# Attention on two head pairs at a time: scores in 64x64 quarters of the array, beside the value products

## The chip, the cores and the metric

The kernel runs on one core of a Trainium2 chip. The metric is device microseconds of that core, the median of the runs of one build. Besides the timed runs there is one profiled execution of the kernel before, from which every row below is taken.

## What is computed

Windowed attention over 4 batches, 8 heads, 576 positions and 64 dimensions a head, then two expert layers, all in float32:

```python
scores = scale * np.matmul(q, k.transpose(0, 1, 3, 2))
mask = (rel >= 0) & (rel < window)            # window = 64
attn = np.exp(scores - max); attn = attn / (sum + 1e-9)
x = np.matmul(attn, v)                        # to [2304 tokens, 512]
h = x @ w_in                                  # 512 -> 2048
x = g(h) @ w_out                              # g piecewise quadratic, 2048 -> 512
h = x @ w_in2                                 # 512 -> 1024
h = h * softmax(h); h = layer_norm(h) * g_ln
out = h @ w_out2                              # 1024 -> 512
```

Here `rel` is query position less key position, so a query sees itself and the 63 keys before it.

## The kernel before

**Attention.** The 2304 tokens are 12 tiles of 192 (`TT`), three to a batch. A tile has four head pairs (`NP`); one tile and one head pair is a group `g`, 48 in all, worked on in order. A tile has three blocks of 64 queries (`QB`); each block sees 128 keys, its own 64 and the 64 before it. The first block of a batch sees only 64 (`first(t, i)`). A group goes through six steps:

- `load_qk` loads queries and keys of one group as 32x32 pieces, four DMAs for each, and `st_qkt` transposes them on VectorE: the keys of both heads go to `kT` (128 partitions, 64 for each head), the queries to `q_diag`, which holds for each query block 64 columns of head 0 in the upper 64 partitions and 64 of head 1 in the lower, and zeros elsewhere. (For the first 12 groups both go through TensorE instead.)
- `st_s` makes the scores of both heads in one product a block: 128 rows of `q_diag` (half of them zeros) against 128 columns of `kT`. VectorE adds the mask and takes the maximum, ScalarE the exponential with its sum.
- `st_norm` divides by the sum. `st_t` transposes the probabilities on TensorE, and ScalarE copies them to SBUF (`pT`).
- `st_v` multiplies by the values: for each block and head a product whose output has 64 partitions, head 0 in the upper and head 1 in the lower half of `ps_x`. ScalarE rounds the result into `xh`, VectorE keeps the rest in `xl`.

**First expert layer.** Blocks `j` of 384 tokens (two tiles), six of them, with 16 steps `f` each. `moe_h` multiplies 12 times into `ps_h` (hidden columns of step `f`), `moe_g` to `moe_g3` make the nonlinearity on ScalarE and VectorE, and `moe_y` multiplies 12 times into four accumulators `acc`, two steps later. All of these products have 384 columns over the full array ("ordinary products" below).

**How they are woven.** Attention runs ahead of the expert layer: each step `f` calls `slot` twice, and `slots` is a generator that yields between the attention's steps. Up to group `GB` = 16 it has one loop, from `GB + 1` on another; both take four slots, two steps `f`, a group. Block 0 of the expert layer takes groups 7 to 16, blocks 1 to 4 take the rest, and the last block runs beside the second layer's start. From block 1 on, `at_bank` and `h_bank` take PSUM banks from one ring of four, so a bank that one step takes must have been read by whoever used it four bank requests earlier. Weights of the first layer are loaded, converted and split during block 0; those of the second layer are converted in blocks 0 to 4. The framework then orders the instructions of each engine from the program's order and its own costs, so the order on an engine is not that of the code.

**What is quoted below.** Float32 products are recorded as two passes, so three score products (`x3`) are six records in the trace; transposes are recorded once.

Of the kernel before, what the change touches and what calls it, by code (L numbers as in the profile page):

```python
# [8 lines left out]
F32 = mybir.dt.float32  # L9
F32R = mybir.dt.float32r  # L10
# [10 lines left out]
def kernel(  # L21
# [28 lines left out]
    NG = NTILES * NP  # L50
    NST = 5
    G0, F0, NC, NQ, NV = 6, 2, 4, 6, 7

    const = ctx.enter_context(tc.tile_pool(name="const", bufs=1))
    dram = ctx.enter_context(tc.tile_pool(name="dram", bufs=1, space=DRAM))
# [51 lines left out]
    def as_f32(a):  # L107
        return a.bitcast(F32)
# [139 lines left out]


    NPE = 3 * NP  # L250
    qn, kn, qk, vw, qT, kT, xh, xl = {}, {}, {}, {}, {}, {}, {}, {}
    sc, pr, sums, pT = {}, {}, {}, {}

# [3 lines left out]
    def load_qk(g):  # L257
        t, hp = divmod(g, NP)
        b, tl = divmod(t, TPB)
        back = 64 if tl else 0  # L260
        if g < NPE:
            for src, dst, tag, r0, n in (
                (q, qn, "wih", tl * TT, TT // 2),
                (k, kn, "wil", tl * TT - back, (TT + back) // 2),
            ):
                for r in range(2):
                    if t < 2:
                        a = w_p.tile([128, 512], F32, tag=f"{tag}{14 - 2 * t + r}", name="qkn")
                    else:
                        a = at_p.tile([128, 512], F32, tag="qk", bufs=5, name="qkn")  # L270
                    dst[t, r] = a[0:n, :]
            for h0, h1 in ((0, 2), (2, H)) if t == 0 else ((0, H),):
                for src, dst, r0, n in ((q, qn, tl * TT, TT // 2), (k, kn, tl * TT - back, (TT + back) // 2)):
                    for r in range(2):
                        nc.sync.dma_start(
                            out=dst[t, r].rearrange("p (h d) -> p h d", h=H)[:, h0:h1],
                            in_=src[b, h0:h1, r0 + r * n:r0 + r * n + n, :].rearrange("h p d -> p h d"),
                        )
            return
        a = at_p.tile([128, 14, 32], F32, tag="qk", bufs=5, name="qk")  # L280
        for src, r0, m0 in ((q, tl * TT, 0), (k, tl * TT - back, 6)):
            n = tl * TT + TT - r0
            for x in range(2):
                s_ = src[b, 2 * hp + x, r0:r0 + n, :].rearrange("(m j) (e i) -> e j m i", j=32, i=32)
                for e in range(2):
                    p0 = 64 * x + 32 * e
                    nc.sync.dma_start(out=a[p0:p0 + 32, m0:m0 + n // 32, :], in_=s_[e])
        qk[g] = a
# [10 lines left out]
            vw[t, i] = w  # L299


    q_diag = [at_p.tile([128, QB, 2, 64], F32, bufs=1, name=f"q_diag{z}") for z in range(2)]
    for z in q_diag:
        nc.vector.memset(z, 0.0)

    def st_qkt(g):
        t, hp = divmod(g, NP)
        qt = qT[g] = q_diag[g % 2]
        kt = kT[g] = at_p.tile([128, TT + 64], F32, tag="kT", name="kT")
        if g >= NPE:  # L310
            a = qk.pop(g)
            for x in range(2):
                s_ = slice(64 * x, 64 * x + 64)
                nc.vector.transpose(qt[s_, :, x, :], a[s_, 0:6, :].rearrange("p m c -> p (m c)"))
            c0 = 0 if t % TPB else 64
            nc.vector.transpose(kt[:, c0:], a[:, 6:14 - c0 // 32, :].rearrange("p m c -> p (m c)"))
            return
        ps = at_bank("ps_t")
        c = 0
        for src in (qn, kn):  # L320
            for r in range(2):
                a = src[t, r]
                n = a.shape[0]
                nc.tensor.transpose(ps[:, c:c + n], a[:, hp * 128:hp * 128 + 128], ident[0:n, 0:n])  # L324
                c += n
        psq = ps[:, 0:TT].rearrange("c (i q) -> c i q", i=QB)
        nc.vector.tensor_copy(qt[0:64, :, 0, :], psq[0:64])
        nc.scalar.copy(qt[64:128, :, 1, :], psq[64:128])
        nc.scalar.copy(kt[:, TT + 64 - (c - TT):], ps[:, TT:c])
# [4 lines left out]
    def st_s(g):  # L334
        t, hp = divmod(g, NP)
        ps = at_bank("ps_s")
        tmp = p = at_p.tile([128, QB, 128], F32, tag="p", bufs=3, name="p")
        mx = at_p.tile([128, QB], F32, tag="mx", name="mx")
        sm = at_p.tile([128, QB], F32, tag="sm", name="sm")
        for i in range(QB):  # L340
            c0 = 64 if first(t, i) else 0
            nc.tensor.matmul(  # L342
                ps[:, i * 128 + c0:i * 128 + 128],
                qT[g][:, i, :, :].rearrange("p x q -> p (x q)"),
                kT[g][:, i * 64 + c0:i * 64 + 128],
                start=True, stop=True,
            )
        for i in range(QB):
            c0 = 64 if first(t, i) else 0
            nc.vector.tensor_tensor_reduce(  # L350
                out=tmp[:, i, c0:], in0=ps[:, i * 128 + c0:i * 128 + 128], in1=mask[:, c0:],
                scale=-0.125, scalar=3.0e38, op0=ALU.add, op1=ALU.min, accum_out=mx[:, i:i + 1],
            )
        for i in range(QB):
            c0 = 64 if first(t, i) else 0
            nc.scalar.activation(  # L356
                p[:, i, c0:], tmp[:, i, c0:], ACTF.Exp, bias=mx[:, i:i + 1], scale=-1.0,
                accum_out=sm[:, i:i + 1],
            )
        pr[g], sums[g] = p, sm  # L360

    def st_norm(g):
        t, hp = divmod(g, NP)
        p, sm = pr[g], sums.pop(g)
# [3 lines left out]
        eng = nc.gpsimd if g < NPE else nc.vector  # L368
        i0 = 0
        if first(t, 0):  # L370
            eng.tensor_tensor(
# [6 lines left out]
            op=ALU.mult,  # L378
        )

    def st_t(g):
        t, hp = divmod(g, NP)
        p = pr.pop(g)
# [12 lines left out]
        pT[g] = o  # L396

    def st_v(g):
        t, hp = divmod(g, NP)
# [15 lines left out]
        c = slice(tj * TT, tj * TT + TT)  # L415
        nc.scalar.copy(xh[j][:, hp, c], ps[:, 0:TT])
        nc.vector.tensor_tensor(xl[j][:, hp, c], ps[:, 0:TT], as_f32(xh[j][:, hp, c]), op=ALU.subtract)  # L417


    hps, gh, gl, acc = {}, {}, {}, {}  # L420
# [96 lines left out]

    GB = TPJ * NP * 2  # L520

    def qkt_and_loads(m):
        if m < NG:
            st_qkt(m)
# [11 lines left out]
    def slots():  # L536
        for g in range(G0 + 1, GB + 1):
# [9 lines left out]
            if g == GB:  # L547
                st_s(g + 1)
            yield
        for g in range(GB + 1, NG + 1):  # L550
            if g == GB + 1:
                st_norm(g)
                qkt_and_loads(g + 1)
            yield
            st_v(g - 1)
            if g < NG:
                st_t(g)
            if g + 1 < NG:
                st_s(g + 1)
            yield  # L560
            if g + 1 < NG:
                st_norm(g + 1)
            v_ahead(g)
            yield
            qkt_and_loads(g + 2)
            yield

    stages = slots()
# [336 lines left out]
```

## Time and profile before

| | |
|---|---|
| median of 3 runs | 718.35 us (717.8 to 719.4) |
| span of the profiled execution, first to last instruction | 717.6 us |
| TensorE busy | 697.3 us, 97% |
| VectorE, ScalarE, GpSimd busy | 455.7, 417.2, 194.3 us |
| granted clock of TensorE, mean over the span | 0.993 |

The profiled execution's own time is given by its span; the timed runs, which also hold what lies before its first and after its last instruction, are 0.2 to 1.8 us above it. Busy time of TensorE is the union of its records, whose ends are modelled; what a product costs in a stream is therefore read from one start to the next. Engines are named PE (TensorE), DVE (VectorE), ACT (ScalarE), POOL (GpSimd) and SP (DMA queue).

### The profile page before, as it was taken

Reading aid. Unit: us, or ns where it says so; the run is one execution under the profiler, and the core shown is the slowest. Engines: PE = TensorE matmul, PEld = TensorE weight load, DVE = VectorE, ACT = ScalarE, POOL = GpSimd, SP = SyncE. Lnnn points to the kernel's source line nnn. Section 1 sums busy time; section 2 is a strip of 40 time slices with the busy share of each in tenths; the row PEclk is TensorE's granted clock in tenths of the full one; section 3 lists DMA queues with packets and bytes.
Section 4 is the critical chain, followed back from the end, with each engine's and each line's share of the span. In section 5 each row is a group of like instructions: output and inputs, shape, how many; then the busy total and the mean of one; then the engine's idle time right before and its main releaser. Section 6 shows DMA issues by size and latency. Waiting matters only on the chain.

```text
span 717.6 us, 12382 instructions
## 1 busy us (share of the span) xinstructions
PE 697.3 (97%) x4259; PEld 640.5 (89%) x4259; DVE 455.7 (64%) x1222; ACT 417.2 (58%) x1021; POOL 194.3 (27%) x217
## 2 busy tenths in 40 slices
PE   7899889999999999999999999999999999999998
PEld 5689878999999999999999999989998888888887
DVE  4549998564556556655566543463368889988850
ACT  5778877555556555666665655454454645545541
POOL 2458877200002000012002101662274132310000
PEclk9989999999999999999999999999999999999999
DMA  9985897624234252336342200644005445553421
GB/s 197 212 241 174 221 244 178 123 63 106 70 78 138 51 127 56 84 96 152 62 117 92 71 30 31 228 140 147 0 19 186 163 162 176 180 171 109 143 74 44
DMA packets 155542, 88.91 MB, mean 124 GB/s; under 512 B 118616, under 2 KB 141400, under 8 KB 155480
## 3 DMA queue, kind: packets, MB, share of 16 engines
q1 hardware_dynamic: 144040, 64.00, 35.3%
q0 software_dynamic: 8704, 19.41, 8.2%
q10 hardware_dynamic: 2736, 4.72, 1.8%
q8 instruction: 33, 0.54, 0.3%
q14 instruction: 29, 0.24, 0.1%
HBM read 63.97 MB, written 24.12 MB: 123 GB/s over the span
## 4 chain that ended last, share of the span: by engine, by line
PE 80%; issue 7%; DVE 6%; POOL 3%; ACT 2%; DMA 1%; SPq 0%; DVEq 0%; POOLq 0%; ACTq 0%
PE ps_h L429 22%; PE acc L460 22%; PE ps_o L746 14%; PE P L631 10%; PE ps_s L342 5%; PE ps_x L409 4%; PE ps_p L390 2%; POOL wil L247 2%; DVE wst L135 1%; DVE wst L134 1%; DVE gl L449 1%; ACT p L356 1%; PE ps_t L324 1%; DMA qk<-in_q_dram 1%; DVE u L444 0%
## 5 line engine op out<-in xcount | busy, mean ns | idle before, releaser
L429 PE MATMUL ps_h<-xh,wih 128*128 128x384 f32 (+1 forms) x392 | 133.3, 340 | 4.0 <-DVE u L444 4.0
L429 PE MATMUL ps_h<-xl,wih 128*128 128x384 f32 (+1 forms) x392 | 132.1, 337 | 1.4 <-DVE xl L417 1.4
L460 PE MATMUL acc<-gl,woh 128*128 128x384 f32 (+1 forms) x392 | 131.2, 336 | 2.0 <-DVE gl L449 1.6
L429 PE MATMUL ps_h<-xh,wil 128*128 128x384 f32 (+1 forms) x392 | 131.7, 336 | 0.0
L460 PE MATMUL acc<-gh,wol 128*128 128x384 f32 (+1 forms) x392 | 129.8, 333 | 0.0
L444 DVE SCALAR_TENSOR_TENSOR u<-u,ps_h 128x384 f32<-128x384 f32 (+1 forms) x98 | 53.3, 544 | 117.1 <-ACT u L439 116.9
L460 PE MATMUL acc<-gh,woh 128*128 128x384 f32 (+1 forms) x392 | 126.7, 342 | 0.0
L438 ACT ACTIVATE u<-ps_h,half 128x384 f32<-128x384 f32 (+1 forms) x98 | 56.1, 574 | 90.7 <-PE ps_h L429 86.9
L429 PEld LDWEIGHTS ps_h<-xh,wih 128*128 128x128 f32 x392 | 75.1, 192 | 5.6 <-DVE u L444 5.0
L445 ACT CAST gh<-u 128x384 fp32r<-128x384 f32 (+1 forms) x98 | 49.7, 507 | 49.3 <-DVE u L444 40.9
L429 PEld LDWEIGHTS ps_h<-xl,wih 128*128 128x128 f32 x392 | 75.2, 192 | 2.2 <-DVE xl L417 2.0
L460 PEld LDWEIGHTS acc<-gl,woh 128*128 128x128 f32 x392 | 73.8, 188 | 3.7 <-DVE gl L449 2.2
L449 DVE TENSOR_TENSOR gl<-u,gh 128x384 fp32r<-128x384 f32 x80 | 54.4, 680 | 35.1 <-ACT gh L445 34.6
L429 PEld LDWEIGHTS ps_h<-xh,wil 128*128 128x128 f32 x392 | 75.1, 191 | 0.0
L460 PEld LDWEIGHTS acc<-gh,wol 128*128 128x128 f32 x392 | 73.7, 188 | 0.1
L460 PEld LDWEIGHTS acc<-gh,woh 128*128 128x128 f32 x392 | 72.4, 188 | 0.5
L631 PE MATMUL P<-wih,x2p 128*128 128x512 f32 x216 | 70.5, 390 | 0.5 <-DVE xo L472 0.5
L356 ACT ACTIVATE p<-p,mx 128x128 f32<-128x128 f32 (+1 forms) x144 | 55.7, 389 | 17.4 <-DVE mx L350 17.4
L746 PE MATMUL ps_o<-woh,wol 128*128 128x512 f32 (+1 forms) x152 | 57.8, 380 | 0.0
L746 PE MATMUL ps_o<-woh,woh 128*128 128x512 f32 (+1 forms) x152 | 57.7, 379 | 0.0
L746 PE MATMUL ps_o<-wol,woh 128*128 128x512 f32 (+1 forms) x152 | 57.5, 378 | 0.0
L439 ACT ACTIVATE u<-u 128x384 f32<-128x384 f32 (+1 forms) x98 | 51.0, 520 | 2.3
(114 smaller groups left out, 1291.2 us busy)
## 6 DMA issues: line engine op xcount, KB each, us to landing
vw<-in_v_dram SPq DMA_DIRECT2D x32, 256.0 KB, 5.0
wst<-in_moe_w_in_dram SPq DMA_DIRECT2D x16, 512.0 KB, 5.0
wst<-in_moe_w_out_dram SPq DMA_DIRECT2D x16, 512.0 KB, 5.0
lnd<-e SPq DMA_DIRECT2D x16, 512.0 KB, 2.7
lT<-lnd SPq DMA_DIRECT2D x64, 128.0 KB, 2.9
x2d<-xo POOLq DMA_DIRECT2D x24, 192.0 KB, 2.3
out_dram<-o ACTq DMA_DIRECT2D x17, 256.0 KB, 2.8
wst<-in_moe_w_in_dram POOLq DMA_DIRECT2D x8, 512.0 KB, 5.5
```

Of the source, the lines that this page charges most:

```text
L342: nc.tensor.matmul(ps[:, i * 128 + c0:i * 128 + 128], qT[g][:, i, :, :].rearrange("p x q -> p (x q)"), kT[g][:, i * 64 + c0:i * 64 + 128], ...
L356: nc.scalar.activation(p[:, i, c0:], tmp[:, i, c0:], ACTF.Exp, bias=mx[:, i:i + 1], scale=-1.0, accum_out=sm[:, i:i + 1],)
L409: nc.tensor.matmul(ps[64 * x:64 * x + 64, i * 64:i * 64 + 64], vw[t, i][0:n, 2 * hp + x, :], o[0:n, i, 64 * x:64 * x + 64], start=True, st ...
L429: nc.tensor.matmul(ps, a, bb[:, kc, c], start=(n == 0), stop=(n == 3 * KC - 1))
L438: nc.scalar.activation(u, ps, ACTF.Relu, bias=half, scale=0.5)
L439: nc.scalar.activation(u, u, ACTF.Square)
L444: g = nc.vector.scalar_tensor_tensor(u, u, 1.0, ps, op0=ALU.min, op1=ALU.max)
L445: return nc.scalar.copy(hi, u).ins, g.ins
L449: eng.tensor_tensor(lo, u, as_f32(hi), op=ALU.subtract)
L460: nc.tensor.matmul(acc[j, e][:, c], a, bb, start=(f == 0 and n == 0 and c.start == 0), stop=(f == NF - 1 and n == 2),)
L631: nc.tensor.matmul(ps, l, r, start=(n == 0), stop=(n == 5))
L746: nc.tensor.matmul(ps, a[kk // 4][:, kk % 4, :], b[kk][:, c:c + w], start=(n == 0), stop=(n == 3 * NK2 - 1),)
```

## The change

From group 18 on (`PU` = 9) two groups, four heads of one tile, are one pair `P`. Keys and queries of a group lie in one buffer `kq`, keys first, and one transpose on VectorE fills both; the queries have no zeros between them any more. `pair_s` makes for each block and head one score product of 64 rows of the array (the head's dimensions) by 64 columns (the block's queries): the head within a group sets the row half and the PSUM bank, the group sets the column half. `pair_v` makes the value products of two groups in one set and writes both groups' `xh` and `xl` at once; its products have the same shape as before. In the new loop of `slots` a pair takes eight slots: values of the pair before and scores of this one in one slot, the normalization, the transposes of queries and keys, and, apart from these, the transposes of the probabilities. Groups up to 17 keep the old steps, in the new buffers.

```diff
+    GB = TPJ * NP * 2
+    PU = GB // 2 + 1
...
-        for src, r0, m0 in ((q, tl * TT, 0), (k, tl * TT - back, 6)):
+        for src, r0, m0 in ((q, tl * TT, 8), (k, tl * TT - back, 2 - back // 32)):
...
+    KQ = TT + 64
+    kq = [at_p.tile([128, 2 * TT + KQ], F32, bufs=1, name=f"kq{z}") for z in range(2)]
+    for z in kq:
+        nc.vector.memset(z[:, 0:2 * TT], 0.0)
 
     def st_qkt(g):
         t, hp = divmod(g, NP)
-        qt = qT[g] = q_diag[g % 2]
-        kt = kT[g] = at_p.tile([128, TT + 64], F32, tag="kT", name="kT")
+        c0 = 0 if t % TPB else 64
+        if g >= 2 * PU:
+            a = qk.pop(g)
+            z = kqT[g] = kq[g % 2][:, 0:KQ + TT]
+            nc.vector.transpose(z[:, c0:], a[:, c0 // 32:, :].rearrange("p m c -> p (m c)"))
...
+    def pair_s(P):
+        t, h2 = divmod(P, NPR)
+        ps = [at_bank("ps_s") for _ in range(2)]
+        mx = at_p.tile([128, 2, QB], F32, tag="mx", name="mx")
+        sm = at_p.tile([128, 2, QB], F32, tag="sm", name="sm")
+        for i in range(QB):
+            c0 = 64 if first(t, i) else 0
+            for c in range(2):
+                z = kqT[2 * P + c]
+                for x in range(2):
+                    r = slice(64 * x, 64 * x + 64)
+                    nc.tensor.matmul(
+                        ps[x][64 * c:64 * c + 64, i * 128 + c0:i * 128 + 128],
+                        z[r, KQ + i * 64:KQ + i * 64 + 64],
+                        z[r, i * 64 + c0:i * 64 + 128],
+                        start=True, stop=True,
+                    )
+        for x in range(2):
+            p = at_p.tile([128, QB, 128], F32, tag="p", bufs=3, name="p")
+            for i in range(QB):
+                c0 = 64 if first(t, i) else 0
+                nc.vector.tensor_tensor_reduce(
+                    out=p[:, i, c0:], in0=ps[x][:, i * 128 + c0:i * 128 + 128], in1=mask[:, c0:],
+                    scale=-0.125, scalar=3.0e38, op0=ALU.add, op1=ALU.min, accum_out=mx[:, x, i:i + 1],
+                )
+            for i in range(QB):
+                c0 = 64 if first(t, i) else 0
+                nc.scalar.activation(
+                    p[:, i, c0:], p[:, i, c0:], ACTF.Exp, bias=mx[:, x, i:i + 1], scale=-1.0,
+                    accum_out=sm[:, x, i:i + 1],
+                )
+            pr[P, x], sums[P, x] = p, sm[:, x, :]
+
+    def pair_v(P):
+        t, h2 = divmod(P, NPR)
+        j, tj = divmod(t, TPJ)
+        if h2 == 0 and tj == 0:
+            xh[j] = wk_p.tile([128, KC, NB], F32R, tag="xh", name="xh")
+            xl[j] = wk_p.tile([128, KC, NB], F32R, tag="xl", name="xl")
+        ps = at_bank("ps_x")[:, 0:2 * TT].rearrange("p (c n) -> p c n", c=2)
+        o = [pT.pop((P, x)) for x in range(2)]
+        for c in range(2):
+            for i in range(QB):
+                n = 64 if first(t, i) else 128
+                for x in range(2):
+                    nc.tensor.matmul(
+                        ps[64 * x:64 * x + 64, c, i * 64:i * 64 + 64],
+                        vw[t, i][0:n, 4 * h2 + 2 * c + x, :],
+                        o[x][0:n, i, 64 * c:64 * c + 64],
+                        start=True, stop=True,
+                    )
+        k2, c = slice(2 * h2, 2 * h2 + 2), slice(tj * TT, tj * TT + TT)
+        nc.scalar.copy(xh[j][:, k2, c], ps)
+        nc.vector.tensor_tensor(xl[j][:, k2, c], ps, as_f32(xh[j][:, k2, c]), op=ALU.subtract)
...
-        for g in range(GB + 1, NG + 1):
-            if g == GB + 1:
-                st_norm(g)
-                qkt_and_loads(g + 1)
-            yield
-            st_v(g - 1)
-            if g < NG:
-                st_t(g)
-            if g + 1 < NG:
-                st_s(g + 1)
-            yield
-            if g + 1 < NG:
-                st_norm(g + 1)
-            v_ahead(g)
-            yield
-            qkt_and_loads(g + 2)
+        st_norm(GB + 1)
+        qkt_and_loads(2 * PU)
+        yield
+        st_v(GB)
+        st_t(GB + 1)
+        qkt_and_loads(2 * PU + 1)
+        yield
+        for P in range(PU, NPP + 1):
+            if P == PU:
+                st_v(GB + 1)
+            else:
+                pair_v(P - 1)
+            if P % NPR == 0:
+                v_ahead(2 * P)
+            if P < NPP:
+                pair_s(P)
+            yield
+            if P < NPP:
+                st_norm(P, 0)
+                st_norm(P, 1)
+            yield
+            qkt_and_loads(2 * P + 2)
+            yield
+            qkt_and_loads(2 * P + 3)
+            yield
+            yield
+            yield
+            if P < NPP:
+                st_t(P, 0)
+                st_t(P, 1)
+            yield
```

On TensorE, before, in block 2 (`ps_x` are value products, `ps_p` transposes of probabilities, `ps_s` scores, `acc` and `ps_h` the ordinary products):

```order
L460 MATMUL acc_2994<-gl,woh_1344 128x384
L460 MATMUL acc_2994<-gh,wol_1345 128x384
L409 MATMUL ps_x<-pT,vw 64x64 x6
L390 MATMUL ps_p<-ident,p 128x128 x3
L342 MATMUL ps_s<-kT,q_diag_124 128x128 x3
L460 MATMUL acc_2991<-gh,woh_1422 128x384
L429 MATMUL ps_h<-xh,wih_168 128x384
```

In the changed program, in block 1, the same engine has the values of one pair and the scores of the next (`kq_124` and `kq_125` are the two groups) between ordinary products:

```order
L496 MATMUL ps_h<-xh,wil_857 128x384
L476 MATMUL ps_x<-pT,vw 64x64 x12
L442 MATMUL ps_s<-kq_124 64x128 x2
L442 MATMUL ps_s<-kq_125 64x128 x2
L442 MATMUL ps_s<-kq_124 64x128 x2
L442 MATMUL ps_s<-kq_125 64x128 x2
L442 MATMUL ps_s<-kq_124 64x128 x2
L442 MATMUL ps_s<-kq_125 64x128 x2
L527 MATMUL acc_2047<-gh,woh_787 128x384
```

and 72 ordinary products later the transposes of that pair, alone:

```order
L496 MATMUL ps_h<-xh,wil_1112 128x384
L402 MATMUL ps_p<-ident,p 128x128 x6
L527 MATMUL acc_2047<-gh,woh_1030 128x384
L527 MATMUL acc_2047<-gl,woh_1030 128x384
L527 MATMUL acc_2047<-gh,wol_1031 128x384
```

So the three kinds of a group, which stood in one set, are two sets for a pair: values with scores, and transposes.

On VectorE, before, one group (`L350` is the masked maximum with its reading out, `L314` and `L316` the transposes, `L366` to `L375` the normalization):

```order
L350 ISA p,mx<-ps_s,mask 128x128
L350 ISA mx 128x1
L314 STREAM_TRANSPOSE q_diag_125<-qk 64x3x64 x2
L316 STREAM_TRANSPOSE kT<-qk 128x256
L366 TENSOR_SCALAR sm<-sm 128x3
L367 RECIPROCAL rs<-sm 128x3
L375 TENSOR_TENSOR p<-p,rs 128x384
```

and in the changed program the last of a pair's six maxima and what follows it (a transpose into `kq_124`, for the next pair, stands ahead of the six):

```order
L452 ISA p,mx<-ps_s,mask 128x128
L452 ISA mx 128x1
L317 STREAM_TRANSPOSE kq_125<-qk 128x448
L377 TENSOR_SCALAR sm<-sm 128x3
L378 RECIPROCAL rs<-sm 128x3
L386 TENSOR_TENSOR p<-p,rs 128x384
L377 TENSOR_SCALAR sm<-sm 128x3
L378 RECIPROCAL rs<-sm 128x3
L386 TENSOR_TENSOR p<-p,rs 128x384
```

Three transposes a group became one, and the normalizations of the pair's two score sets stand together.

## Rows read from the trace of the kernel before

**Rows 1.** The page: busy us (share of the span) and instructions of an engine.

```profile
PE 697.3 (97%) x4259; PEld 640.5 (89%) x4259; DVE 455.7 (64%) x1222; ACT 417.2 (58%) x1021; POOL 194.3 (27%) x217
```

**Rows 2.** Windows: PE, PEld, DVE, ACT, POOL busy, granted clock, DMA share, GB/s.

```profile
60.00:110.00 50.00, 44.20 (x281) 40.24 (x280) 49.37 (x97) 38.73 (x94) 38.78 (x28) 0.97 0.88 234
110.00:445.00 335.00, 334.96 (x2300) 321.42 (x2300) 190.60 (x623) 202.10 (x540) 50.43 (x65) 1.00 0.38 90
```

**Rows 3.** The page: the chain that ended last, by engine.

```profile
PE 80%; issue 7%; DVE 6%; POOL 3%; ACT 2%; DMA 1%; SPq 0%; DVEq 0%; POOLq 0%; ACTq 0%
```

**Rows 4.** Timeline of PE near 430 us: start, us, and how many records follow each other.

```profile
429.51 0.34 PE L460 MATMUL acc<-gh,wol 128*128 128x384 f32 x1
429.78 0.57 PE L409 MATMUL ps_x<-pT,vw 128*64 128x64 f32 x12
430.28 0.55 PE L390 MATMUL ps_p<-ident,p 128*128 128x128 f32 x3
430.67 0.83 PE L342 MATMUL ps_s<-kT,q_diag 128*128 128x128 f32 x6
431.25 0.42 PE L460 MATMUL acc<-gh,woh 128*128 128x384 f32 x1
431.51 0.34 PE L429 MATMUL ps_h<-xh,wih 128*128 128x384 f32 x1
...
437.58 0.33 PE L460 MATMUL acc<-gh,woh 128*128 128x384 f32 x1
...
439.49 0.34 PE L460 MATMUL acc<-gh,wol 128*128 128x384 f32 x1
439.76 0.57 PE L409 MATMUL ps_x<-pT,vw 128*64 128x64 f32 x12
```

**Rows 5.** Timeline of PE, only 208.02 to 208.08: a full set of values begins.

```profile
208.03 0.28 PE L409 MATMUL ps_x<-pT,vw 128*64 128x64 f32 x2
```

**Rows 6.** Timeline of PE, only 227.06 to 227.12: one value product alone begins.

```profile
227.08 0.27 PE L409 MATMUL ps_x<-pT,vw 64*64 64x64 f32 x1
```

**Rows 7.** Timeline of PE near 307 us: a set that ordinary products cut in two.

```profile
306.69 0.34 PE L409 MATMUL ps_x<-pT,vw 128*64 128x64 f32 x4
306.95 0.44 PE L460 MATMUL acc<-gh,woh 128*128 128x384 f32 x1
307.24 0.34 PE L460 MATMUL acc<-gl,woh 128*128 128x384 f32 x1
...
308.22 0.45 PE L409 MATMUL ps_x<-pT,vw 128*64 128x64 f32 x8
308.61 0.55 PE L390 MATMUL ps_p<-ident,p 128*128 128x128 f32 x3
```

**Rows 8.** Timeline of PE: values of a batch's first tile, the first product of 64 rows.

```profile
218.00 0.71 PE L409 MATMUL ps_x<-pT,vw 64*64 64x64 f32 x12
218.65 0.30 PE L388 MATMUL ps_p<-ident,p 128*64 128x128 f32 x1
```

**Rows 9.** Groups of 120 to 445 us: count, busy us, mean ns, idle before.

```profile
L356 ACT ACTIVATE p<-p,mx 128x128 f32<-128x128 f32 x90 | 35.2, 392 | 9.2 <-DVE mx L350 9.2
L314 DVE STREAM_TRANSPOSE q_diag<-qk 64x192 f32<-64x192 f32 x62 | 23.0, 370 | 1.0
L350 DVE CUSTOM_DVE_ANT_0 p<-ps_s,mask 128x128 f32<-128x128 f32 x90 | 21.6, 287 | 10.7 <-PE ps_s L342 10.7
L356 ACT ACTIVATION_READ_ACCUMULATOR p<-p,mx 128x1 f32 x99 | 18.5, 187 | 0.0
...
L375 DVE TENSOR_TENSOR p<-p,rs 128x384 f32<-128x384 f32 x24 | 13.4, 558 | 0.8
...
L316 DVE STREAM_TRANSPOSE kT<-qk 128x256 f32<-128x256 f32 x23 | 10.3, 446 | 0.7
...
L350 DVE DVE_READ_ACCUMULATOR2_ANT mx<- 128x1 f32 x99 | 8.3, 84 | 0.0
...
L367 DVE RECIPROCAL rs<-sm 128x3 f32<-128x3 f32 x33 | 5.8, 176 | 1.1
```

More of the change, by code (lines that the diff above doesn't have):

```diff
@@ L250 @@
     NPE = 3 * NP
-    qn, kn, qk, vw, qT, kT, xh, xl = {}, {}, {}, {}, {}, {}, {}, {}
-    sc, pr, sums, pT = {}, {}, {}, {}
+    NPR = NP // 2
+    NPP = NTILES * NPR
+    qn, kn, qk, vw, qT, kT, kqT, xh, xl = {}, {}, {}, {}, {}, {}, {}, {}, {}
+    pr, sums, pT = {}, {}, {}
     def load_qk(g):
@@ L299, in load_v @@
             vw[t, i] = w
-    q_diag = [at_p.tile([128, QB, 2, 64], F32, bufs=1, name=f"q_diag{z}") for z in range(2)]
-    for z in q_diag:
-        nc.vector.memset(z, 0.0)
+    KQ = TT + 64
+    kq = [at_p.tile([128, 2 * TT + KQ], F32, bufs=1, name=f"kq{z}") for z in range(2)]
+    for z in kq:
+        nc.vector.memset(z[:, 0:2 * TT], 0.0)
     def st_qkt(g):
         t, hp = divmod(g, NP)
-        qt = qT[g] = q_diag[g % 2]
-        kt = kT[g] = at_p.tile([128, TT + 64], F32, tag="kT", name="kT")
+        c0 = 0 if t % TPB else 64
[3 more added lines that the diff above has]
+            nc.vector.transpose(z[:, c0:], a[:, c0 // 32:, :].rearrange("p m c -> p (m c)"))
+            return
+        qt = qT[g] = kq[g % 2][:, 0:2 * TT].rearrange("p (i x q) -> p i x q", i=QB, x=2)
+        kt = kT[g] = kq[g % 2][:, 2 * TT:]
         if g >= NPE:
@@ L313, in st_qkt @@
                 s_ = slice(64 * x, 64 * x + 64)
-                nc.vector.transpose(qt[s_, :, x, :], a[s_, 0:6, :].rearrange("p m c -> p (m c)"))
-            c0 = 0 if t % TPB else 64
-            nc.vector.transpose(kt[:, c0:], a[:, 6:14 - c0 // 32, :].rearrange("p m c -> p (m c)"))
+                nc.vector.transpose(qt[s_, :, x, :], a[s_, 8:14, :].rearrange("p m c -> p (m c)"))
+            nc.vector.transpose(kt[:, c0:], a[:, c0 // 32:8, :].rearrange("p m c -> p (m c)"))
             return
@@ L337, in st_s @@
         tmp = p = at_p.tile([128, QB, 128], F32, tag="p", bufs=3, name="p")
-        mx = at_p.tile([128, QB], F32, tag="mx", name="mx")
-        sm = at_p.tile([128, QB], F32, tag="sm", name="sm")
+        mx = at_p.tile([128, 2, QB], F32, tag="mx", name="mx")[:, 0, :]
+        sm = at_p.tile([128, 2, QB], F32, tag="sm", name="sm")[:, 0, :]
         for i in range(QB):
@@ L360, in st_s, with st_norm @@
         pr[g], sums[g] = p, sm
-    def st_norm(g):
-        t, hp = divmod(g, NP)
-        p, sm = pr[g], sums.pop(g)
+    def st_norm(g, u=None):
+        t = (g if u is None else 2 * g) // NP
+        u = g if u is None else (g, u)
+        p, sm = pr[u], sums.pop(u)
         rs = at_p.tile([128, QB], F32, tag="rs", name="rs")
@@ L367, in st_norm @@
         nc.vector.reciprocal(rs, sm)
-        eng = nc.gpsimd if g < NPE else nc.vector
+        eng = nc.gpsimd if t < 3 else nc.vector
         i0 = 0
@@ L379, in st_norm, with st_t @@
         )
-    def st_t(g):
-        t, hp = divmod(g, NP)
-        p = pr.pop(g)
+    def st_t(g, u=None):
+        t = (g if u is None else 2 * g) // NP
+        u = g if u is None else (g, u)
+        p = pr.pop(u)
         ps = at_bank("ps_p")
@@ L395, in st_t @@
         nc.scalar.copy(o[:, i0:, :], ps[:, i0 * 128:QB * 128].rearrange("p (i c) -> p i c", c=128))
-        pT[g] = o
+        pT[u] = o
     def st_v(g):
@@ L515 @@
     del spare[:]
-    GB = TPJ * NP * 2
     def qkt_and_loads(m):
```

## The prediction

> **What bounds the kernel now.** I read the totals first: TensorE is busy 697.3 of 717.6 us, the other engines between 27% and 64% [rows 1]. Then the stretches: from 110 to 445 us, where blocks 1 to 4 of the first expert layer run beside the attention of the later tiles, TensorE is busy 334.96 of 335 us at a granted clock of 1.00 (the upper level, 2.4 GHz), while VectorE works 57% and ScalarE 60%; only 60 to 110 us looks different, with VectorE busy 49.4 of 50 [rows 2]. The chain that ended last agrees: 80% of it is TensorE [rows 3]. So inside 110 to 445 us a microsecond taken from TensorE's own stream is a microsecond of the kernel, until another engine comes late.
>
> What a group (one tile, two heads) costs there is read from starts in the timeline, since ends are modelled. Ordinary 384-column products start 0.1736 us apart (437.58 to 439.49, eleven steps). From one group's value products to the next, 429.78 to 439.76, are 9.98 us with 48 such products, 8.33 us; the attention takes the other **1.65 us** [rows 4]. Its pieces, start to start: the last ordinary product before the values holds 0.27, so the way in costs 0.10; the twelve value records (six products, each recorded as two passes) 0.50; three transposes 0.39; six score records 0.58, of which five steps of 0.11 and 0.03 before the next product may start; and that product's successor comes after 0.26, 0.09 late [rows 4].
>
> **What the quarters may do is already half visible.** A score product is 128 columns wide and a step of 0.11; a value product has 64 columns and writes half of the output partitions. Where a whole set of value products is queued, two records have begun within 0.06 us [rows 5]; where one product stands alone, only one has, so its two passes follow each other and the pair in the full set is two heads in two column halves of the array at once [rows 6]. The cut set gives the step: four records take 0.26, eight 0.39, twelve 0.50 [rows 4, 7], so a further pair costs about 0.06; with 64 of the scores' columns at 0.055 I take 0.058 for a round of two. What the trace does not show is a product in the lower half of the rows beside one in the upper half; that is the open price.
>
> **The change, part by part, on TensorE, for a pair (what two groups were).**
> Values: 24 records instead of twice 12, in one set. One way in, 0.10. The set costs 0.50 for six rounds and the way out, and six rounds more at 0.058: 0.85.
> Scores: zeros are no longer multiplied, so a pair has 12 products of 64 rows by 64 columns of the array, 24 passes of 128 columns, where two groups had 12 passes over the full array. If four run at once these are six rounds of 0.11. They follow the values directly, and this is a change from 128 rows to 64. Such a change is visible where the first 64 keys of a batch make a value product of 64 rows: the set then takes 0.65 instead of 0.50 [rows 8], so 0.15 for one switch, the same as the 0.15 by which the short set of four records (0.26) exceeds its two rounds (0.11) [rows 7]. Scores with their way out: 0.66 + 0.15 = 0.81. The next ordinary product's successor is late, 0.29 instead of 0.17 after such an exit [rows 7]: 0.11.
> Transposes: six between ordinary products, all full array, so 5 x 0.11 + 0.03 + 0.09 = 0.67 [rows 4]; a first one that cost a switch would add 0.10.
> Sum 0.10 + 0.85 + 0.81 + 0.11 + 0.67 = **2.54 us, against 2 x 1.65 = 3.30**: 0.76 less, and 15 pairs (groups 18 to 47): **11.4 us**.
> The order of the changed program has no set cut by ordinary products any more; now four groups are cut, each at 0.10 + (0.26 + 0.39 - 0.50) + 0.11 = 0.36 [rows 4, 7]: **1.4 us** gained. The four pairs at the start of a batch have three inner switches (64, 128, 64, 128 rows) where their eight groups have one each, and shorter scores in both: 4 x (0.45 - 0.11) - 8 x (0.15 - 0.11) = **1.0 us** lost.
> Together 11.8 us. The profiled execution's span is 717.6; the median of the runs, 718.35, lies 0.75 above it, for what is outside first and last instruction; the sum is taken from that: 718.35 - 11.8 = **706.5 us**.
>
> **What is costed at nothing, and its cover.**
> VectorE loses two transposes of 0.370 and one of 0.446 a group and gets one of 448 columns, an estimate of 0.65 from the two widths; the reductions, normalizations and their count stay [rows 9]. It gains some 16 us of idle time that nothing waits for. The added wait stands there: the transposes for the next pair have one buffer per group and must wait until the scores have read it. Behind them on VectorE stand the six reductions, which need those scores anyway, so nothing that could run is held. From the scores' end to the six transposes the new order has 72 ordinary products, 12.5 us. In it must pass: a transpose 0.65, six reductions of 0.287 + 0.084, six exponentials of 0.392 + 0.187 that run behind them, and two normalizations of 0.558 and 0.176 with a small step ahead, about 0.9 [rows 9]; with one exponential still to come after the last reduction that is 0.65 + 2.2 + 0.6 + 1.8 = 5.3 us, and some 8 with the ordinary work of ScalarE in between. Were the cover gone, each microsecond late would cost 15.
> PSUM: scores now hold two of the four banks of the ring. The bank that the values take was that of an ordinary set ended 24 products and six transposes earlier, 24 x 0.1736 + 0.6 = 4.8 us, in which ScalarE and VectorE pass over it three times. Loads: each group keeps its 8 DMAs, issued two groups together and four groups ahead, which is two pairs of 96 x 0.1736 + 2.54 = 19.2 us. One large cast for the two groups replaces two. The order also moves some of VectorE's weight work between 60 and 110 us, where it is full; the set of instructions is the same, and I give it 1 us either way.
>
> **A rule against.** The value rounds of 0.058 leave nothing for loading weights beside 0.055 for the columns, so those loads pass beside running products of the same rows [rows 4, 7]. The Trainium skill, "TensorE: Matmul & The Clock Gate", section "Part 3: Packing small matmuls", says that weight loads overlap running matmuls only when the row group differs; by it, each round would pay its load. The trace does not agree for column halves; for quarters it is a rival (c) below.
>
> **Rivals.** (a) Four at once: 706.5, own range 703 to 710: rounds of 0.10 to 0.14, a quarter more for the four starts (six rounds, 15 pairs: -0.9 to +2.7), one switch nil or doubled (15 x 0.15 = 2.2 either way), and the 1 us between 60 and 110. For it: two halves already run so, and the two row halves write different banks.
> (b) The change doesn't do what it says: row halves take turns, two at a time. Six rounds more, 6 x 0.11 x 15 = 9.9: 716.4, a hair faster. For it: no row of this trace shows two row halves.
> (c) Every round also pays a load of 64 columns, bounded by the columns' own 0.055: 6 x 0.055 x 15 = 5.0, 711.5. Against it: the rounds of values.
> (d) Slower: the quarters run one after another on the path. 24 rounds, 18 more than in (a): 18 x 0.11 x 15 = 29.7, 736.2. It turns to a loss when the 24 passes need more than 13 rounds (11.8 / 15 = 0.79, seven rounds). Against it: the 0.06 us in which two records start [rows 5].
> (e) A wait takes over: the transposes find their probabilities late by half a microsecond: 7.5 us, 714.0. Against it: 12.5 us of cover for 5 to 8.
>
> **Chances.** (a) 0.73, (b) 0.10, (c) 0.05, (d) 0.06, (e) 0.06. The time forecast is that of (a). 703 to 712 holds (a), (c) and half of (e); (b), (d) and the rest of (e), 0.19, stay outside. With 0.2% (1.4 us) as what a measurement here can tell from no change, (a), (c), most of (e) and half of (b) are faster, 0.87; the other half of (b) is the same, 0.06; (d) is slower, 0.07.
>
> **What would show it.** In the changed profile, a pair in blocks 1 to 4: 24 value records and 24 score records start to start about 0.85 and 0.8 us; one of scores alone near 0.8 means four at once, 1.5 two at once, 2.7 one at a time. Four score records begun within some 0.06 us would settle it directly. The six transposes should take 0.6 with no idle ahead of them; TensorE should stay busy through the stretch, which ends some 12 us earlier, and what follows should last as long as before. The prediction is wrong if score records start in twos or singly, if a switch between values and scores costs much more than 0.15, or if TensorE idles ahead of the transposes or the values.

## The result and the profile after

The changed kernel takes **710.84 us** (median of four runs, 710.16 to 712.67) where the kernel before takes 718.2 beside it (four runs, 717.8 to 719.4): a ratio of 0.9899, 95% interval 0.9883 to 0.9915. That is 7.4 us of the 11.8 forecast, inside the range. The profiled execution is the longest of the four, with a span of 710.9 us against 717.6. The page's first line, which answers to [rows 1]:

```profile
PE 685.6 (96%) x4439; PEld 630.0 (89%) x4439; DVE 434.3 (61%) x1147; ACT 413.0 (58%) x1006; POOL 195.3 (27%) x217
```

TensorE has 180 passes more (zeros gone, but twice as many score products) and is busy 11.7 us less.

**The stage that the change is about.** The windows that answer to [rows 2] (PE, PEld, DVE, ACT, POOL busy, granted clock, DMA share, GB/s):

```profile
60.00:110.00 50.00, 43.21 (x280) 38.62 (x280) 47.04 (x98) 40.11 (x96) 40.10 (x30) 1.00 0.91 234
110.00:445.00 335.00, 333.86 (x2555) 322.44 (x2554) 177.19 (x554) 201.50 (x533) 52.87 (x70) 1.00 0.40 95
```

From 110 to 445 us TensorE is still the bound, idle for 1.1 us of 335. VectorE is busy 13.4 us less, since the groups that answer to [rows 9], here of 120 to 435 us, now hold one transpose a group, 0.638 us as against an estimate of 0.65, while a reduction takes what it did (0.281 us, before 0.287):

```profile
L317 DVE STREAM_TRANSPOSE kq<-qk 128x448 f32<-128x448 f32 x22 | 14.0, 638 | 0.0
```

The timeline of PE at one pair, which answers to [rows 4] (start, us, and how many records follow each other), and the six transposes of the same pair:

```profile
296.38 0.34 PE L496 MATMUL ps_h<-xh,wil 128*128 128x384 f32 x1
296.65 0.92 PE L476 MATMUL ps_x<-pT,vw 128*64 128x64 f32 x24
297.50 0.89 PE L442 MATMUL ps_s<-kq 64*64 64x128 f32 x24
298.32 0.44 PE L527 MATMUL acc<-gh,woh 128*128 128x384 f32 x1
298.60 0.33 PE L527 MATMUL acc<-gl,woh 128*128 128x384 f32 x1
...
310.92 0.82 PE L402 MATMUL ps_p<-ident,p 128*128 128x128 f32 x6
311.50 0.42 PE L527 MATMUL acc<-gh,woh 128*128 128x384 f32 x1
311.75 0.34 PE L527 MATMUL acc<-gl,woh 128*128 128x384 f32 x1
```

Start to start: way in 0.27 (0.10 beyond an ordinary product), values 0.85, scores 0.82, next product 0.28 (0.11 late). The same timeline narrowed to 297.490 to 297.525, and then to 297.49 to 297.77, counts the scores that have begun:

```profile
297.50 0.34 PE L442 MATMUL ps_s<-kq 64*64 64x128 f32 x4
...
297.50 0.45 PE L442 MATMUL ps_s<-kq 64*64 64x128 f32 x8
```

Four begin within 0.035 us: the four quarters do run at once. The first round holds 0.16 us and the next four 0.11 each; from the last round to the next product are 0.22.

**Where the gain went.** Each product of the expert layers exists in both programs, so the difference of its starts says how far ahead the changed program is at that point. Three such points carry the account: the product at 120.77 us in the kernel before (ahead of it both programs have done the same attention work), the first output product of the second layer, `ps_o`, at 548.23, and the end. Rows of the timeline of PE, first of the kernel before, then of the changed one:

```profile
120.77 0.34 PE L429 MATMUL ps_h<-xh,wih 128*128 128x384 f32 x1
548.23 0.39 PE L746 MATMUL ps_o<-woh,woh 128*128 128x512 f32 x1
```

```profile
121.91 0.34 PE L496 MATMUL ps_h<-xh,wih 128*128 128x384 f32 x1
536.87 0.41 PE L826 MATMUL ps_o<-woh,woh 128*128 128x512 f32 x1
```

| stretch | forecast | first profile | second profile |
|---|---|---|---|
| start to 120.77 | 0, 1 either way | -1.1 | -0.9 |
| 120.77 to 548.23, the pairs | +11.8 | +12.5 | +12.4 |
| 548.23 to the end, the second layer | 0 | -4.7 | -2.7 |
| span | 11.8 | 6.7 | 8.7 |

(Both profile columns are differences to the first profile of the kernel before; the last one is from the first experiment below.) The pairs bring what was forecast and 0.6 more. The rest is lost outside the pairs.

**The loss at the end.** The waits of PE from 535 to 600 us, of the kernel before and of the changed one (what waited, for what; us in total, times, longest):

```profile
PE P L631 <- DVE xo L472: 0.5, 1, 0.5
```

```profile
PE ps_o L826 <- DVE wol L814: 2.9, 2, 2.2
```

The chain behind the longer wait is read from the timelines of SP, POOL, DVE and PE. In the second layer each group of 128 rows is normalized on VectorE, with one small power on GpSimd (`stat`, L775), written to memory (`lnd`, L792), read back transposed (`lT`, L794) and split on VectorE (`wol`, L814) for `ps_o`. For each two row groups SyncE also loads the next inputs (`x2r`, L666), from which GpSimd makes sums (`xs`, L680).

```profile
553.58 0.34 SPq L792 DMA_DIRECT2D lnd<-e  x1
557.32 1.76 SPq L794 DMA_DIRECT2D lT<-lnd  x4
559.19 0.43 SPq L666 DMA_DIRECT2D x2r<-x2d  x1
560.45 0.34 SPq L792 DMA_DIRECT2D lnd<-e  x1
```

```profile
564.70 1.46 POOL L680 TENSOR_TENSOR xs<-x2r 128x256 f32<-128x256 f32 x2 [10.42 <-DMA x2r<-x2d]
...
566.81 0.55 POOL L775 TENSOR_TENSOR stat<-stat,mhalf 128x1 f32<-128x1 f32 x1
```

```profile
567.40 1.22 DVE L779 TENSOR_SCALAR s<-s,stat 128x1024 f32<-128x1024 f32 x1 [4.91 <-POOL stat L775]
568.54 1.28 DVE L814 TENSOR_TENSOR wol<-lT,woh 128x512 fp32r<-128x512 f32 x2
```

```profile
566.72 0.39 PE L711 MATMUL P<-wih,x2p 128*128 128x512 f32 x1
569.27 0.50 PE L826 MATMUL ps_o<-woh,wol 128*128 128x512 f32 x1 [2.17 <-DVE wol L814]
```

In the kernel before, SyncE issued the same write, the load and the next write at these times, and the first two landed after 2.6 and 4.2 us:

```profile
564.11 0.34 SPq L712 DMA_DIRECT2D lnd<-e  x1
...
568.66 0.38 SPq L586 DMA_DIRECT2D x2r<-x2d  x1
570.98 0.34 SPq L712 DMA_DIRECT2D lnd<-e  x1
```

```profile
lnd<-e SPq DMA_DIRECT2D x1, 512.0 KB, 2.6
...
x2r<-x2d SPq DMA_DIRECT2D x1, 512.0 KB, 4.2
```

Read the changed kernel's chain backwards: PE waits for `wol`, which stands on VectorE behind a step that waits for `stat`; `stat` stands on GpSimd behind `xs`; `xs` waits for the load `x2r`, which SyncE could issue only after four reads that wait for the write `lnd` to land. The DMA view of 553.5 to 553.9 shows the first thing that is unusual:

```profile
q8 instruction: 1, 0.02, 19.5%
...
lnd<-e SPq DMA_DIRECT2D x1, 512.0 KB, 3.7
```

One 16 KB packet of an instruction queue begins 0.24 us after the write's issue, and the write lands after 3.7 us, 1.1 later than before. The two transfers behind it are late in turn and meet each other: `x2r` and the next `lnd` are issued 1.26 us apart and land after 5.4 each (before: 2.32 apart, 4.2 and 3.2).

The stall costs more than itself. The window behind it:

```profile
570.70:574.20 3.50, 3.50 (x10) 2.68 (x10) 3.44 (x7) 0.82 (x2) 0.55 (x1) 0.51 0.36 150
```

After 2.2 us of idle TensorE works on for 1.4 us at a granted clock of 1.00 and then for 3.5 us at 0.51, the lower level, where products start 0.43 us apart instead of 0.23: another 1.6 us. From 574.2 to 576 the clock is 1.00 again.

### The profile page after: what moved, and what is told of

The parts are those of the page before. It is cut to its first block, busy times and chain, and to the rows that moved or that the text cites. A ratio compares the mean times of both kernels' runs of the same rounds, so it can differ in the third digit from the quotient of the medians.

```text
span 710.9 us, 12663 instructions
## 1 busy us (share of the span) xinstructions
PE 685.6 (96%) x4439; PEld 630.0 (89%) x4439; DVE 434.3 (61%) x1147; ACT 413.0 (58%) x1006; POOL 195.3 (27%) x217
## 4 chain that ended last, share of the span: by engine, by line
PE 72%; DVE 10%; issue 7%; POOL 4%; DMA 3%; ACT 2%; SPq 1%; DVEq 0%; POOLq 0%; ACTq 0%
PE ps_h L496 22%; PE acc L527 22%; PE ps_o L826 13%; PE P L711 7%; PE ps_x L476 2%; PE ps_p L402 2%; PE ps_s L442 2%; PE ps_s L352 2%; DVE wst L137 2%; POOL wil L249 2%; DVE wst L136 1%; PE ps_x L421 1%; DMA wst<-in_moe_w_out_dram 1%; DVE gl L516 1%; DVE s L740 1%
## 5 line engine op out<-in xcount | busy, mean ns | idle before, releaser
L516 DVE TENSOR_TENSOR gl<-u,gh 128x384 fp32r<-128x384 f32 x80 | 52.8, 661 | 37.3 <-ACT gh L512 36.7
L711 PEld LDWEIGHTS P<-wih,x2p 128*128 128x128 f32 x216 | 40.5, 188 | 9.2 <-DVE xo L539 0.9
```

The costliest lines, as they stand in the source:

```text
L516: eng.tensor_tensor(lo, u, as_f32(hi), op=ALU.subtract)
L711: nc.tensor.matmul(ps, l, r, start=(n == 0), stop=(n == 5))
```

## The experiments

**Twice the same.** Both kernels again, unaltered.

> The changed kernel once more, unaltered, timed again and profiled a second time. Theory (the tail's loss of 4.65 us between 541 and 569 us is set off by two small transfers that happen to land late, 3.67 and 5.35 us after their issue where the kernel before has 2.62 and 3.19): the time is again 710 to 711.5, and the second profile either has the same two late landings and TensorE's two stalls of 0.7 and 2.2 us at the tail's products, which would make it a property of this program, or has them elsewhere or shorter, which would make it chance, with a span nearer to 708. Rival (the tail's loss follows from the order of the instructions): stalls of the same place and size whatever the landings are.

> The kernel before, profiled a second time, as a measure for the tail: from about 545 us on its TensorE should wait 0.5 us in all, as in the first profile, if its tail is undisturbed by nature, and the two landings should again be 2.6 and 3.2 us. If stalls of 1 to 3 us turn up here too, the tail varies from one execution to the next in both kernels and the loss isn't the change's.

The changed kernel took 711.21 us against 719.12 (ratio 0.9894, 0.9878 to 0.9910), and its second profile waits at the same place:

```profile
PE ps_o L826 <- DVE wol L814: 2.5, 2, 1.7
```

The write issued at 553.62 lands after 3.1 us, `x2r` after 5.5, with the instruction packet at 553.72. This time the stall of 1.7 us is not followed by a lower clock, which is why the tail loses 2.7 us and not 4.7. The second profile of the kernel before has a span of 717.3 and waits 0.8 us in this stretch. So the loss is a property of the program; the clock behind it is not there every time.

**The loads on another queue.** The row loads of the tail, all but the first two pieces, go to GpSimd's queue, in both kernels:

```diff
+        eng = nc.gpsimd if p >= 2 else nc.sync
...
-            nc.sync.dma_start(out=r[:, :, c:c + n], in_=x2d[j]...)
+            eng.dma_start(out=r[:, :, c:c + n], in_=x2d[j]...)
```

> The changed kernel, with the row loads of the tail (the reloads of the transposed residual, for all but the first two pieces) issued from GpSimd's queue, so that they no longer stand behind SyncE's wait for the write of the normalized rows. Theory (the tail's loss is one late landing that holds SyncE, and with it the next load): the stalls of 0.7 and 2.2 us at TensorE go, and with them 3 to 4 us: 707 to 708. Rival (the loss comes from the tail's chain on GpSimd and VectorE itself, or from an instruction load): no change, 710.8 within 1 us, since the rows only come earlier to an engine that is late for another reason.

> The same edit in the kernel before, whose tail shows no stall of TensorE: no change, 718.2 within 0.7 us, under both theories. If this one gains 3 us too, the tail of the kernel before had a hidden wait as well, and the tail's 4.65 us is no loss of the change.

The gain forecast for the changed kernel did not come: 711.23 us (0.9894, as unaltered), the number of the rival. The kernel before, forecast unaltered, got slower, 722.83 (1.0050, 1.0036 to 1.0063). The load now leaves at 557.69 instead of 559.19, but takes 6.0 us from that queue in both kernels, so GpSimd starts its sums at 563.85, 0.85 us earlier. The edit swaps one lateness for another; it neither shows the first one's cause nor bears out the rival.

**Moving the instruction packet.** The trace has one 16 KB instruction packet for every 128 passes of TensorE. Dummy products put ahead of TensorE's first transposes, in the 2.7 us in which it waits for the first load, shift the later packets; behind them the traces show every instruction of TensorE, VectorE, ScalarE and GpSimd in the same order as without them:

```diff
     w_load(3)
+    ps_w = h_bank()
+    for _ in range(8):
+        nc.tensor.matmul(ps_w[0:1, 0:1], half, half, start=True, stop=True)
     st_qkt(0)
```

> The changed program with eight one-element products (16 passes) put ahead of TensorE's first transposes, in the 2.7 us in which TensorE waits for the first load. The trace shows one 16 KB packet of an instruction queue for every 128 passes of TensorE; in both profiles of the changed kernel one runs at 553.7 to 555.1 us, beside the write of the normalized rows issued at 553.6, which lands after 3.1 to 3.7 us where the kernel before has 2.6. Sixteen passes move it to about 549, where no transfer runs. Theory (the late landing is that packet's doing, and TensorE's second stall in the tail follows from it): the write lands after 2.6 to 2.7, the second stall of 1.7 to 2.2 us at the tail's products shrinks below 0.7, and the time is 708.5 to 709.7. Rival (chance or the tail's own order): landings, stall and time as they are, 711.

> The kernel before with sixteen one-element products (32 passes) in the same place. There the instruction packets of the tail run at 549 and 578.5 us, clear of the writes; 32 passes earlier one comes to about 570.7, beside a write of normalized rows and the load ahead of it. Theory: that write or load lands 0.5 to 1 us later than its 2.6 and 4.2, and the kernel before gets a stall of TensorE in its tail of 0.5 to 2 us: 719.5 to 721. Rival: no change, 719 within 0.5.

> The changed program with four one-element products (8 passes) ahead of TensorE's first transposes. Theory (where the tail's instruction packet falls decides): 8 passes put it at about 551.9 us, 1.7 us before the write of normalized rows is issued and over before its data move; the write lands in 2.6 to 2.7, the second stall is below 0.7, time 709 to 710, as with 16 passes. Rival (16 passes helped by something else, such as a warmer start): half the help, 710.3, or none, 711.

> The changed program with twelve one-element products (24 passes) ahead. Theory: the tail's packet at about 547.3, where no transfer runs, so the stall of 553 to 572 us is gone here too; the next packet then comes at about 580.3, beside the write of a later row group issued at 579.6 to 580.0, whose rows have more slack: 709 to 710.5, the upper end if that write's delay reaches TensorE. Rival (a warmer start helps): the same or less than 709.4 whatever the packets do.

| kernel | packet begins | write lands after | `x2r` lands after | PE waits 535 to 600 | time, ratio |
|---|---|---|---|---|---|
| changed | 0.24 after the write's issue | 3.7 | 5.4 | 2.9 | 710.84, 0.9899 |
| changed, again | 0.10 after | 3.1 | 5.5 | 2.5 | 711.21, 0.9894 |
| 8 passes | 0.25 ahead of it | 2.7 | 4.8 | 1.0 | 709.62, 0.9873 |
| 16 passes | 0.73 ahead | 2.6 | 4.3 | 0.4 | 709.37, 0.9864 |
| 24 passes | 5.8 ahead | 2.6 | 4.5 | 0.5 | 709.06, 0.9864 |
| before | none near | 2.6 | 4.2 | 0.5 | 718.2 |
| before, 32 passes | 0.42 ahead of `x2r` | 2.6 | 6.6 | 3.4 | 720.87, 1.0024 |

The intervals are 0.9855 to 0.9890 for 8 passes, 0.9851 to 0.9878 for 16 and 24, 1.0015 to 1.0032 for the kernel before with 32. The packets came out otherwise than forecast with 8 and 16 passes (at 553.33 and 552.96 instead of 551.9 and 549), but the write's own data begin only at 554.4 to 554.5 us. The packet of the 16-pass version ends at 553.9 and the write lands on time; that of the 8-pass version ends at 554.2 and the write is still 0.1 late. With 16 passes:

```profile
553.69 0.34 SPq L795 DMA_DIRECT2D lnd<-e  x1
...
558.24 0.38 SPq L669 DMA_DIRECT2D x2r<-x2d  x1
```

```profile
570.70:574.20 3.50, 3.50 (x17) 2.88 (x17) 3.50 (x9) 0.59 (x1) 0.00 (x0) 1.00 0.48 175
```

SyncE is 0.95 us earlier at `x2r`, and where the changed kernel ran ten products at half the clock, seventeen run. In the kernel before, the same trick moves a packet beside `x2r`, which then lands 2.4 us later (forecast: 0.5 to 1), and makes a stall of 2.3 us:

```profile
x2r<-x2d SPq DMA_DIRECT2D x1, 512.0 KB, 6.6
```

```profile
PE ps_o L749 <- DVE wol L737: 2.9, 2, 2.3
```

Help in one kernel, harm in the other, by the same dummy work: the place of the packet it is. The tail from 548.23 on then loses 1.1 (8 passes), 0.4 (16) and 0.6 us (24) instead of 2.7 to 4.7. The version with 24 passes, 709.06 us, is the fastest of all, 2 us below the changed kernel.

**Without the quarters.** The same pairs and sets, but scores over the whole array, with the zeros. (The transposes of queries and keys go back to the zeroed layout with it, and the value products take the probabilities by group; those lines are left out here.)

```diff
-            for c in range(2):
-                z = kqT[2 * P + c]
-                for x in range(2):
...
+            for c in range(2):
+                g = 2 * P + c
+                nc.tensor.matmul(ps[c][:, i * 128 + c0:i * 128 + 128],
+                    qT[g][:, i, :, :].rearrange("p x q -> p (x q)"),
+                    kT[g][:, i * 64 + c0:i * 64 + 128], start=True, stop=True)
```

> The changed program with everything but the quarters: pairs, one set of values and scores, transposes apart, but the scores of a group again as three products over the whole array with the zeros in them (12 passes a pair instead of 24, the queries transposed into the zeroed layout as before the change). Theory (the quarters are worth six rounds of 0.11 against twelve, less the switch and the late successor that they add): scores 1.35 instead of 0.81, no switch, 0.5 us a pair more in blocks 1 to 4, so some 7 to 8 us of the 12.7 measured there are given back, 718 to 719; the other 4.6 are the sets put together. Rival (the gain is that of fewer and larger sets, the quarters bring little): 711 to 713.

715.30 us, ratio 0.9950 (0.9935 to 0.9965). By the three points: the pairs' stretch gains 4.4 us instead of 12.4 to 12.6, so the quarters are worth **8.1 us** and the larger sets 4.4, as the theory had it. The time is lower than its 718 to 719: this program's tail loses nothing (its packets, at 547.2 and 574.7 us, fall clear of the write at 559.6 and the load at 564.2), and it reaches the product of 120.77 on time. Its scores, in the timeline of PE:

```profile
299.59 0.92 PE L469 MATMUL ps_x<-pT,vw 128*64 128x64 f32 x24
300.44 1.60 PE L435 MATMUL ps_s<-kq 128*128 128x128 f32 x12
301.80 0.42 PE L520 MATMUL acc<-gh,woh 128*128 128x384 f32 x1
```

1.36 us for twelve passes, against 0.82 for 24 in quarters.

**Quarter by quarter.** The same products in another order of writing:

```diff
-        for i in range(QB):
-            for c in range(2):
-                for x in range(2):
+        for c in range(2):
+            for x in range(2):
+                for i in range(QB):
```

> The changed program with the same 12 score products of a pair written quarter by quarter (three products of one quarter, then the next quarter) instead of round robin over the four. Theory (a quarter's product starts when its own quarter is free, but in the order of the queue): while the first quarter's six passes follow each other the other three idle, so a pair's scores take 18 to 24 steps of 0.11 instead of six, 1.3 to 2.0 us more for each of 15 pairs: 730 to 741. Rival (each quarter has a queue of its own and takes its products whatever stands ahead for others): no change, 711.

719.01 us, ratio 1.0003 (0.9992 to 1.0014): neither. A pair's scores take 1.63 us instead of 0.82 (302.22 to 303.85 below), and the pairs' stretch gains 2.3 us instead of 12.4. (This program's tail loses 1.4 us, which is not the scores'.) The timeline up to 302.495, up to 302.51, and whole:

```profile
302.22 0.54 PE L442 MATMUL ps_s<-kq 64*64 64x128 f32 x3
...
302.22 0.59 PE L442 MATMUL ps_s<-kq 64*64 64x128 f32 x4
...
302.22 1.69 PE L442 MATMUL ps_s<-kq 64*64 64x128 f32 x24
303.85 0.45 PE L527 MATMUL acc<-gh,woh 128*128 128x384 f32 x1
```

The first quarter's passes start at 302.22, 302.38 and 302.49; within 0.02 us of the third comes a fourth, which can't be the same quarter's, whose passes are 0.11 apart. So a later product overtakes the three passes that its neighbour still has to run, but not more than these: the next quarter begins when the one ahead begins its second product. The order of writing decides, with a little slack. The record has no list of the queue's own order for this run, so that the framework kept the written order is inferred. For it: in this pair the first quarter's third product starts ahead of the second quarter's second (302.71 and 302.77), while in the pair at 202.25, whose first products are half as wide, it starts behind it (202.64 and 202.59); no one order with every start in turn gives both, and in both the next quarter begins 0.006 us after the second product of the one ahead.

**Pairs later.** Groups 18 to 25 are done one by one as before, pairs start at the 27th group:

```diff
-    PU = GB // 2 + 1
+    PU = GB // 2 + 5
```

> The changed program with the pairs starting at the 27th group instead of the 19th: the groups between are done one by one as before the change. Theory (the 1 to 1.7 us that the changed kernel loses between 64 and 121 us come from the order in which the groups before the first pair are put between the products): the product that starts at 120.77 in the kernel before starts within 0.4 of that again, instead of 0.4 to 1.1 later; four of 15 pairs are given up, 4 x 0.85 = 3.4, so the start of the last layer's first output product is 11.4 - 3.4 + 1.3 = 9.3 us ahead of the kernel before. Rival (the loss is that of VectorE's order further ahead, in block 0, where the joined buffer for queries and keys already moves its transposes): that product 0.4 to 1.1 late as before, and 8 us ahead at the end. The time itself hangs on where the tail's instruction packets fall, 711 to 714.

714.63 us (0.9941, 0.9927 to 0.9956). The product of 120.77 starts at 120.70, as the theory has it, but it was 1.1 us ahead at 64 us and loses 1.0 on the way, as the changed kernel does, with the same waits. The eleven pairs bring 8.1 us up to the product of 444.83, where fifteen bring 11.3: 0.8 a pair, as forecast. Then this program has a stall of its own at the end of the first layer:

```profile
PE P L723 <- DVE stat L752: 3.0, 1, 3.0
```

behind which the clock is 0.71 from 530 to 533 us, so the forecast of 9.3 ahead became 5.4. On block 0 it decides nothing: the start of the product fits the theory, the loss on the way to it the rival.

## Why the prediction was right, and where it was off

**The number.** 710.84 us lies inside the range, but that is not the forecast coming true: the mechanism (a) was priced at 706.5 with 703 to 710 as its own range, and by the number alone (c), 711.5, fits better. The traces decide for (a), and two losses outside the pairs make the difference.

**The quarters.** Four at once, in rounds of 0.11, as forecast: four score records in 0.035 us, and 8.1 us by the run without them. Rival (b), row halves taking turns, and (d), one after another, are out. So is (c): 24 score passes in 0.82 us leave no room for a load in each round; only the first round is longer, by 0.05. The rule of the Trainium skill ("TensorE: Matmul & The Clock Gate", "Part 3: Packing small matmuls") that weight loads overlap running products only where the row group differs is not borne out: twelve value rounds, all of the same rows, take 0.85 us here with the way out. The same section says that products start strictly in the order of the queue; the run written quarter by quarter doesn't agree, if the queue holds the written order: there a quarter's first product starts while three passes written ahead of it have yet to start.

**The sum for a pair.** Forecast 0.10 + 0.85 + 0.81 + 0.11 + 0.67 = 2.54; measured 0.10, 0.85, 0.82, 0.11 and 0.66. The 0.15 for a switch from 128 rows to 64, taken from the short sets of a batch's start, has the right size, but it does not stand at that switch: values take 0.85 whether quarters or, in the run without quarters, whole-array scores follow. It is 0.05 in the first round of scores and 0.11 on the way out of them. With the cut sets and the batches' first pairs the stretch was to gain 11.8 and gained 12.4 to 12.6 in the five profiles that have these pairs and their loads unaltered.

**What was costed at nothing.** Cover held for VectorE, for the transposes (no idle ahead of them) and for the PSUM banks; rival (e) did not come.

**Block 0.** "1 us either way" was too little, and one-sided: nine profiles of changed programs reach the product of 120.77 between 0.1 us early and 1.75 late (mean 0.85 late), four of the kernel before and its variants between on time and 1.3 early (mean 0.6 early), so some 1.4 us are lost. The spread comes from ahead of 65 us: from the product of 64.98 us to that of 120.77 all nine changed programs lose time, 0.7 to 1.9 us, and the four others gain or lose 0.1 at most. The waits of PE from 60 to 125 us, before and after:

```profile
PE ps_h L429 <- DVE u L444: 4.0, 4, 1.7
PE ps_p L388 <- DVE p L371: 1.3, 2, 1.1
PE acc L460 <- POOL gl L449: 0.4, 1, 0.4
```

```profile
PE ps_h L496 <- DVE u L511: 3.1, 5, 1.3
PE ps_p L400 <- DVE p L382: 2.8, 2, 1.7
PE acc L527 <- POOL gl L516: 0.9, 2, 0.4
PE ps_x L421 <- ACT pT L407: 0.8, 1, 0.8
PE ps_s L352 <- DVE xl L429: 0.4, 1, 0.4
```

The waits change places and grow by 2.3 us. What makes them is left open: VectorE's order is new here, and TensorE's is too, since up to this product it runs the same 717 passes in another order.

**The step that failed** is "what follows should last as long as before". The order of the tail is the same, but its place among the instruction packets is not: 180 passes more ahead of it put a packet beside a write that SyncE waits for, and the chain behind that write has little slack: 0.5 us later, TensorE waits 2.5 instead of 0.4. That took 2.7 us, 4.7 with the lower clock, and explains most of the difference between 7.4 and 11.8; block 0 takes the rest, and the pairs give 0.6 back. Clear of the packet the change is worth 9.6 to 9.9 us (ratio 0.9864).

## What to carry to other kernels

Small products that use half the rows and half the columns paid off here in quarters when they were written round robin over the quarters, and not quarter by quarter; the price of a stretch can be summed from starts in the timeline, term by term, to a few hundredths of a microsecond. Write the ledger by starts of the same product in both programs before explaining a time: it shows at once whether the changed stage or another one moved. A stage that another engine's queue holds together can lose by a change far ahead of it, so a gain should be timed with one or two harmless shifts of the instruction stream before it is judged.

## What had not been expected of the hardware

- Instruction packets are transfers like others. One of 16 KB takes 0.9 to 2.1 us in these traces, and there is about one for every 128 passes of TensorE (33 for 4259, 35 for 4439); beside a write of 512 KB it delayed its landing by 0.5 to 1.1 us. The Trainium skill, "DMA: Bandwidth & Descriptors", section "Queues, rings and completion order", says that each DMA engine takes turns between its queues by whole packets; a write whose last piece waits for one such packet on one engine would agree with that. The traces don't say on which DMA engine a packet ran, so this is not shown.
- A stall of 2.2 us of TensorE was followed, 1.4 us after its end, by 3.5 us at half the clock; one of 1.7 us at the same place was not, nor was one of 2.3 us in the kernel before with 32 passes (1.00 from 580 to 584.5 us), and one of 3.0 us in another program was. The length of the stall alone does not tell.
- Products of different quarters overtake each other: with quarters written in blocks, in the order as far as it is known, the next quarter starts 0.27 us after the one ahead, at its third pass, and not after its sixth.
